# An attention and MLP kernel without its dummy matmuls, with attention re-paced and the users of v casts held back

## The chip, the cores and the metric

The kernel runs on one core of a Trainium2 chip. The metric is device time in microseconds. Every execution listed here is of state "fast", and each came with the span of the core and the mean granted TensorE clock. Before the change: 347.17 us, the median of 3 runs (346.78 to 348.75) that were known when the prediction was made.

## The reference, cut to what matters

Attention over 8 batches of 8 heads, 576 queries, head size 64, with 16 extra "beacon" keys before the 576 causal ones. Its output, as 4608 tokens of 512 numbers, goes through an MLP with a squared ReLU.

```python
# q, k, v: (8, 8, 576, 64); beacon_k, beacon_v: (8, 8, 16, 64)
scores = scale * q @ concat(beacon_k, k).T        # causal on the last 576 keys
a = softmax(scores)
x = (a @ concat(beacon_v, v)).transpose(0, 2, 1, 3).reshape(4608, 512)
h = x @ w_in                                      # 512 -> 2048
g = maximum(h, 0) ** 2
return g @ w_out                                  # 2048 -> 512
```

## The kernel before

The kernel does not write its instructions by hand in order. It lists operations with a modelled duration, dependencies and a priority. A small simulation of time (`Order.run`) then picks, for each engine, which ready operation comes next. Only the resulting order reaches the chip. A modelled number therefore never makes the chip wait; it only decides what stands before what.

Attention works on 32 pairs of heads: pair p belongs to batch p // 4. The MLP works on 9 chunks of 512 tokens. Chunk j can start once the attention of batch (512 (j+1) - 1) // 576 is normalised and transposed into `xT`: for batches 0 to 2 by TensorE, for batches 3 to 7 by a DMA transpose on the queue of SP. Other names in the traces: `stg` holds what was just loaded from memory; a cast turns it into bf16 (`vb` for v, `qk_area` for q and k); `qT` and `kT` are q and k transposed; `strip` holds scores, `pt` their exp, `xn` the normalised output before its transpose.

Dummy matmuls fill TensorE where the model has it idle before 22 us:

```python
    FILL_UNTIL = 22.0
    # ... in run(), when no operation is ready for engine e:
                    if best is None:
                        if e == "PE" and 0.3 < now < self.FILL_UNTIL and self.pools["ps"]:
                            cols = 128 if now < 4.0 else 256
                            free[e] = now + 0.107
                            issued.append((Op("fill", "PE", 0.107, ...
```

Attention is paced against the MLP. `progress` is the MLP's modelled TensorE time so far. A pair's scores may be issued only when it has reached a share of a chunk for each pair; if nothing else is ready, the gate is ignored (`fallback`):

```python
    mlp_chunk_us = 27.7
    LEAD, PACE = -0.4, 0.255
        def gate(o):
            if p < HP:
                return True
            return o.progress >= mlp_chunk_us * (LEAD + PACE * (p - HP))
```

`late` holds back TensorE's users of an operation in the model, because loads can be later on the chip than in it:

```python
        cast[b, x, c] = add(f"cast{b}{x}{c}", engs, ..., emit_cast, ...,
                            late=2.0 if x == "v" and b > 0 else 0.0)
        trans[b, x] = [add(f"tr{b}{x}", "SP", 4.1, emit, ..., dma=3.7, late=3.0)]
            o = add(f"xt{b}.{t}", "SP", 1.32, emit, ..., dma=0.64 * n / 128, late=0.5)
```

The softmax here doesn't subtract the row's maximum and nothing guards it: scores larger than these inputs give would overflow.

Of the kernel before, what the change touches and what calls it, by code (L numbers as in the profile page):

```python
# [45 lines left out]
class Order:  # L46
# [2 lines left out]

    LAT = {"PE": 0.2, "ACT": 0.2, "DVE": 0.15, "POOL": 0.25, "SP": 0.1, "-": 0.0}  # L50

    FILL_UNTIL = 22.0
    DEPTH = {"SP": 4, "ACT": 8, "POOL": 8}
    DMA_LAT = {"SP": 0.6, "ACT": 0.6, "POOL": 2.0}

# [7 lines left out]
    def add(self, *a, **kw):  # L63
        op = Op(*a, **kw)
        op.need = [d for d in op.need if d is not None]
        self.ops.append(op)
        return op

    def run(self):
        engines = ["PE", "ACT", "DVE", "POOL", "SP", "-"]  # L70
        for op in self.ops:
            op.left = len(op.need) + len(op.behind)
            for d in op.need:
                d.users.append(op)
            for d in op.behind:
                d.followers.append(op)
        avail = {e: [] for e in engines}

        def release(op):
            for e in op.engs:  # L80
                avail[e].append(op)

        for op in self.ops:
            if op.left == 0:
                release(op)
        free = {e: 2.3 if e == "DVE" else 0.0 for e in engines}
        dma_free = 0.0
        lanes = {"SP": [], "POOL": [], "ACT": []}
        events = [(0.0, 0, None, None)]
        seq = 0  # L90
        started = set()
        issued = []
        now = 0.0
        while events:
            now = events[0][0]
            while events and events[0][0] <= now + 1e-9:
                _, _, kind, op = heapq.heappop(events)
                if kind in ("done", "done_pe"):
                    for u in op.users:
                        if ("PE" in u.engs) == (kind == "done_pe"):  # L100
                            u.left -= 1
                            if u.left == 0:
                                release(u)
                elif kind == "give":
                    from_op, which = op.give if isinstance(op.give, tuple) else (op.give, 0)
                    pool, cls = from_op.take[:2]
                    self.pools[pool].append(from_op.slots[which])
                    if cls in self.inuse:
                        self.inuse[cls] -= 1
            again = True  # L110
            while again:
                again = False
                for e in engines:
                    if free[e] > now + 1e-9:
                        continue
                    best = None
                    fallback = None
                    for op in avail[e]:
                        if any(free[x] <= now + 1e-9 for x in op.engs[:op.engs.index(e)]):
                            continue  # L120
                        if op.take:
                            pool, cls, need = op.take
                            if len(self.pools[pool]) < need:
                                continue
                            if cls in self.limits and self.inuse[cls] + need > self.limits[cls]:
                                continue
                        if op.gate is not None and not op.gate(self):
                            if fallback is None or op.prio < fallback.prio:
                                fallback = op
                            continue  # L130
                        if op.dma and len(lanes[e]) >= self.DEPTH[e] and lanes[e][-self.DEPTH[e]] > now + 1e-9:
                            continue
                        if best is None or op.prio < best.prio:
                            best = op
                    if best is None:
                        best = fallback
                    if best is None:
                        if e == "PE" and 0.3 < now < self.FILL_UNTIL and self.pools["ps"]:
                            cols = 128 if now < 4.0 else 256
                            free[e] = now + 0.107  # L140
                            issued.append((Op("fill", "PE", 0.107, lambda e, cols=cols, bank=self.pools["ps"][0]: self.fill(bank, cols)), e, now))
                            seq += 1
                            heapq.heappush(events, (free[e], seq, "free", None))
                        continue
                    op = best
                    started.add(id(op))
                    for u in op.followers:
                        u.left -= 1
                        if u.left == 0:
                            release(u)  # L150
                    for ee in op.engs:
                        avail[ee].remove(op)
                    if op.take:
                        pool, cls, need = op.take
                        op.slots = [self.pools[pool].pop(0) for _ in range(need)]
                        op.held = (pool, cls, op.slots[0])
                        if cls in self.inuse:
                            self.inuse[cls] += need
                    dur = op.dur[e] if isinstance(op.dur, dict) else op.dur
                    end = now + dur  # L160
                    free[e] = end
                    self.progress += op.pe_time
                    issued.append((op, e, now))
                    seq += 1
                    heapq.heappush(events, (end, seq, "free", op))
                    if op.dma:
                        dma_free = max(dma_free, now + self.DMA_LAT[e]) + op.dma
                        seen = max(end, dma_free + 1.6)
                        lanes[e].append(seen)
                        seq += 1  # L170
                        heapq.heappush(events, (seen, seq, "free", op))
                    else:
                        seen = end + self.LAT[e]
                    seq += 1
                    heapq.heappush(events, (seen, seq, "done", op))
                    seq += 1
                    heapq.heappush(events, (seen + op.late, seq, "done_pe", op))
                    if op.give is not None:
                        seq += 1
                        heapq.heappush(events, (seen, seq, "give", op))  # L180
                    again = True
        assert len(started) == len(self.ops), [o.name for o in self.ops if id(o) not in started][:20]
        for op, e, _ in issued:
            if e != "-":
                op.insts = op.emit(e)
                for d in op.sync:
                    for x in op.insts:
                        self.wait_for(x, d.insts[-1])
        self.issued = issued
        return now  # L190
# [3 lines left out]
def kernel(  # L194
# [11 lines left out]
    nc = tc.nc  # L206
# [17 lines left out]
    def sb(name, shape, dt):  # L224
        return pool.tile(shape, dt, name=name)
# [41 lines left out]
    g = [sb(f"g{i}", [128, NFT, TCH], BF16) for i in range(2)]  # L267
# [4 lines left out]
    ps = [psum.tile([128, 512], FP32, name=f"ps{i}") for i in range(4)]  # L272

    def wait_for(later, first):
# [3 lines left out]
    order = Order(  # L278
        pools={"strip": range(2), "ps": range(4), "stg": range(NSTG), "pt": range(NPT)},
        limits={"av": 2, "tp": 2},  # L280
    )
    order.wait_for = wait_for

    def emit_fill(bank, cols):
        nc.tensor.matmul(ps[bank][:, 0:cols], g[1][:, 0, 0:128], g[1][:, 0, 0:cols], start=True, stop=True)  # L285

    order.fill = emit_fill

    add = order.add

    nc.vector.memset(g[1][:, 0, 0:256], 0.0)
    nc.vector.memset(warm, 0.0)  # L292
    for i in range(2):
        nc.vector.memset(kT[i][:, :, Nb + S:NT * 128], 0.0)
# [54 lines left out]
    def add_load(b, x, c, prio, behind=[], sync=[]):  # L349
# [34 lines left out]
        if x != "v":  # L384
            if b < NPE + 2:
                deps += [zero_ops[b]]
            else:
# [1 line left out]
        engs = ("POOL", "DVE") if b == 0 and c <= 1 else ("POOL",)  # L389
        cast[b, x, c] = add(f"cast{b}{x}{c}", engs, {"DVE": 0.6, "POOL": 0.65}, emit_cast,  # L390
                            prio=prio if b else prio - 220.0, deps=deps, give=ld,
                            late=2.0 if x == "v" and b > 0 else 0.0)

    def add_trans(b, x, prio):
        srcb, dst = (qb, qT) if x == "q" else (kb, kT)
# [57 lines left out]
    def add_strided(b, prio):  # L453
# [7 lines left out]
        for part, (t0, np_, ns, prs) in enumerate(parts_of[b]):  # L461
            n_tok = np_ * ns
            own = b == 0 and part < 2
            for pr in prs:
                groups = ["kq"] if 2 * n_tok <= 1024 else ["k", "q"]
                for n, xs in enumerate(groups):
                    box = {}

                    def emit_tp(e, xs=xs, pr=pr, box=box, part=part, np_=np_, ns=ns, n_tok=n_tok, own=own, prs=prs):
                        pp = ps[box["t"].held[2]].bitcast(BF16)  # L470
                        for i, x in enumerate(xs):
                            for u in range(ns):
# [6 lines left out]
                                                        strided_buf(b, x, part)[:, 2 * (pr - prs[0]) + hj, u, :],  # L479
                                                        ident[0:np_, 0:np_])  # L480

                    tp = add(f"tp{b}.{part}.{pr}{xs}", "PE", 0.1 + (0.055 if b == 0 else 0.075) * ns * len(xs), emit_tp,
                             prio=100.0 * (HP * b + pr) - (190 if b else 1190 if part == 0 else 1090) + 0.1 * n,
                             deps=[strided[b, part, pr, x] for x in xs] + [ident_op], take=("ps", "tp"))
                    box["t"] = tp
# [95 lines left out]
        return SPLIT if p < NSPLIT else WHOLE  # L581

    mlp_chunk_us = 27.7
    LEAD, PACE = -0.4, 0.255
    norm_ops = {}

    def add_pair(b, pr):
# [291 lines left out]
    late = []  # L879
    for b in range(B):  # L880
# [3 lines left out]
        if b < NPE:  # L884
            add_strided(b, lp - 200.0 if b == 0 else lp)
# [31 lines left out]
        if b >= 1:  # L917
            for j in late:
                add_chunk(j)
            late = []  # L920
# [48 lines left out]
```

## Time and profile before

| what | before | where it is read |
|---|---|---|
| median of the runs | 347.17 us | the runs |
| span of the profiled execution | 347.5 us | the page |
| TensorE busy | 334.9 us, 96% | the page, part 1 |
| waits for xT | 0.57 and 1.92 us | waits, timeline |
| half clock in the middle | 3.41 us | clock records, windows |
| dummy matmuls | 71, 10.6 us busy | the page, part 5 |

The page of the kernel before: TensorE in 40 slices (tenths busy), its granted clock in tenths, and the chain of work that ended last by engine and by line.

```profile
PE   8899999999999999999999998999999999999995
...
PEclk9999999999999999999999999899999999999999
...
PE 83%; DMA 6%; DVE 3%; POOL 3%; SPq 2%; issue 1%; ACT 1%; ACTq 0%; POOLq 0%; DVEq 0%
PE ps L805 34%; PE ps L840 33%; PE ps L674 8%; PE strip L622 7%; DMA stg<-in_v_dram 4%; DMA xT<-xn 2%; POOL qk_area L443 1%; PE ps L742 1%; SPq L365 1%; DVE pt L648 1%; DVE pt L651 1%; SPq L725 1%; PE ps L478 1%; POOL vb L320 0%; DVE xn L694 0%
```

Two thirds of the chain are the two MLP matmul lines, L805 (x times w_in) and L840 (g times w_out). TensorE is what the kernel is made of, so a gain can only come from its holes. One slice of the clock row shows an 8.

The waits of TensorE before (who waited for what: us in total, times, longest):

```profile
PE ps L805 <- DMA xT<-xn: 2.5, 2, 1.9
...
PE ps L674 <- POOL vb L320: 0.8, 3, 0.4
```

The timeline of TensorE before, around the longest of them (start, busy time, engine, line, shapes and count; in brackets the idle time before it and what ended that):

```profile
213.53 0.63 PE L674 MATMUL ps<-vb,pt 128*128 128x65 bf16 x15
214.09 0.58 PE L622 MATMUL strip<-qT,kT 64*128 64x496 bf16 x4
214.60 1.04 PE L840 MATMUL ps<-w_out,g 128*128 128x512 bf16 x4
217.55 3.55 PE L805 MATMUL ps<-xT,w_in 128*128 128x512 bf16 x8 [1.92 <-DMA xT<-xn]
221.03 0.48 PE L622 MATMUL strip<-qT,kT 64*128 64x336 bf16 x8
```

TensorE sits idle for 1.92 us until xT of batch 5 lands. Then eight matmuls take 3.55 us. The windows view before shows why. Its columns are the stretch, its length, the busy time of PE, PEld, DVE, ACT and POOL with their counts, the granted clock (PEclk), the DMA share and GB/s.

```profile
214.12:217.54 3.42, 1.52 (x10) 0.41 (x9) 1.38 (x3) 2.07 (x3) 0.99 (x2) 1.00 1.39 97
217.54:220.95 3.41, 3.40 (x8) 1.00 (x8) 0.69 (x1) 0.00 (x0) 0.00 (x0) 0.50 0.68 190
220.95:224.36 3.41, 3.36 (x22) 1.63 (x23) 2.48 (x5) 2.61 (x5) 0.00 (x0) 1.00 1.10 228
```

A stretch of 3.42 us with TensorE busy for 1.52 us is followed by 3.41 us at half clock, and that by full clock again.

The start before, in TensorE's timeline: one group of 24 attention-times-v matmuls, and the first MLP matmuls.

```profile
19.75 0.91 PE L674 MATMUL ps<-vb,pt 128*128 128x65 bf16 x24
...
24.19 0.57 PE L805 MATMUL ps<-xT,w_in 128*128 128x240 bf16 x4
```

### The profile page before, as it was taken

Reading aid. Unit: us, or ns where it says so; the run is one execution under the profiler, and the core shown is the slowest. Engines: PE = TensorE matmul, PEld = TensorE weight load, DVE = VectorE, ACT = ScalarE, POOL = GpSimd, SP = SyncE. Lnnn points to the kernel's source line nnn. Section 1 sums busy time; section 2 is a strip of 40 time slices with the busy share of each in tenths; the row PEclk is TensorE's granted clock in tenths of the full one; section 3 lists DMA queues with packets and bytes.
Section 4 is the critical chain, followed back from the end, with each engine's and each line's share of the span. In section 5 each row is a group of like instructions: output and inputs, shape, how many; then the busy total and the mean of one; then the engine's idle time right before and its main releaser. Section 6 shows DMA issues by size and latency. Waiting matters only on the chain.

```text
span 347.5 us, 7286 instructions
## 1 busy us (share of the span) xinstructions
PE 334.9 (96%) x2916; PEld 179.9 (52%) x2957; DVE 169.0 (49%) x366; ACT 193.9 (56%) x293; POOL 92.2 (27%) x144
## 2 busy tenths in 40 slices
PE   8899999999999999999999998999999999999995
PEld 7578765444554544444458743444444454444442
DVE  6696974258436862467246733473256412301300
ACT  3787764377656744576437644475467616615611
POOL 9674803316315515210423054021000000000000
PEclk9999999999999999999999999899999999999999
DMA  8999979999999999698989999990520032011002
GB/s 143 207 206 211 205 122 203 235 213 214 200 229 217 220 196 210 144 208 134 206 137 238 223 210 154 225 210 2 106 85 2 0 104 87 2 60 61 2 24 97
DMA packets 143664, 51.70 MB, mean 149 GB/s; under 512 B 130670, under 2 KB 138382, under 8 KB 143630
## 3 DMA queue, kind: packets, MB, share of 16 engines
q1 hardware_dynamic: 135231, 42.25, 61.7%
q0 software_dynamic: 7904, 8.69, 14.8%
q8 instruction: 23, 0.38, 0.5%
q10 hardware_dynamic: 495, 0.30, 0.3%
q14 instruction: 11, 0.09, 0.1%
HBM read 37.22 MB, written 9.44 MB: 134 GB/s over the span
## 4 chain that ended last, share of the span: by engine, by line
PE 83%; DMA 6%; DVE 3%; POOL 3%; SPq 2%; issue 1%; ACT 1%; ACTq 0%; POOLq 0%; DVEq 0%
PE ps L805 34%; PE ps L840 33%; PE ps L674 8%; PE strip L622 7%; DMA stg<-in_v_dram 4%; DMA xT<-xn 2%; POOL qk_area L443 1%; PE ps L742 1%; SPq L365 1%; DVE pt L648 1%; DVE pt L651 1%; SPq L725 1%; PE ps L478 1%; POOL vb L320 0%; DVE xn L694 0%
## 5 line engine op out<-in xcount | busy, mean ns | idle before, releaser
L805 PE MATMUL ps<-xT,w_in 128*128 128x512 bf16 (+3 forms) x689 | 134.6, 343 | 3.3 <-DMA xT<-xn 2.5
L840 PE MATMUL ps<-w_out,g 128*128 128x512 bf16 x550 | 130.5, 379 | 1.8 <-issue 0.8
L637 ACT ACTIVATE pt<-strip 128x832 bf16<-128x832 f32 (+4 forms) x128 | 103.9, 863 | 28.9 <-PE strip L622 28.4
L805 PEld LDWEIGHTS <-w_in 128*128 128x128 bf16 x704 | 65.3, 98 | 59.2 <-issue 9.4
L821 ACT ACTIVATE g<-ps 128x512 bf16<-128x512 f32 (+2 forms) x123 | 68.4, 556 | 45.9 <-PE ps L805 45.0
L840 PEld LDWEIGHTS <-g 128*128 128x128 bf16 x576 | 52.5, 98 | 61.8 <-issue 4.4
L830 DVE TENSOR_TENSOR g<-g 128x1024 bf16<-128x1024 bf16 (+2 forms) x80 | 51.0, 642 | 58.6 <-ACT g L821 57.2
L318 ACT COPY osb<-ps 128x512 f32<-128x512 f32 x32 | 18.8, 586 | 66.5 <-PE ps L840 45.6
L320 POOL CAST qk_area<-stg 128x512 bf16<-128x512 f32 (+2 forms) x60 | 39.5, 665 | 59.0 <-DMA stg<-in_k_dram 39.1
L320 POOL CAST vb<-stg 128x512 bf16<-128x512 f32 (+1 forms) x39 | 26.6, 693 | 78.0 <-DMA stg<-in_v_dram 57.1
L674 PEld LDWEIGHTS <-pt 128*128 128x128 bf16 (+1 forms) x960 | 37.1, 97 | 15.6 <-issue 3.9
L674 PE MATMUL ps<-vb,pt 128*128 128x65 bf16 (+1 forms) x960 | 40.5, 194 | 2.0 <-POOL vb L320 0.8
L648 DVE TENSOR_TENSOR pt<-pt,tri 128x1024 bf16<-128x1024 bf16 (+1 forms) x36 | 24.6, 686 | 29.9 <-ACT pt L637 29.9
L622 PE MATMUL strip<-qT,kT 64*128 64x80 bf16 (+6 forms) x400 | 35.0, 277 | 0.2 <-DMA kT<-qk_area 0.2
L692 DVE RECIPROCAL rcp<-ps 128x5 f32<-128x5 f32 (+2 forms) x64 | 12.3, 193 | 41.8 <-PE ps L674 41.5
L694 DVE TENSOR_TENSOR xn<-ps,rcp 128x320 bf16<-128x320 f32 (+2 forms) x64 | 31.5, 492 | 2.3
L823 DVE TENSOR_SCALAR g<-ps 128x512 bf16<-128x512 f32 (+2 forms) x37 | 23.4, 632 | 16.1 <-PE ps L805 14.7
L622 PEld LDWEIGHTS <-kT 64*128 64x128 bf16 x400 | 11.9, 94 | 18.0 <-issue 13.9
L651 DVE TENSOR_TENSOR pt<-pt,tri 80x160 bf16<-80x160 bf16 x32 | 12.2, 383 | 0.0
L285 PE MATMUL ps<-g 128*128 128x256 bf16 (+1 forms) x71 | 10.6, 298 | 1.1 <-DVE warm L292 1.1
L365 POOL DMA_DIRECT2D stg<-in_v_dram x10 | 8.5, 852 | 4.9 <-DMA w_in<-in_moe_w_in_dram 3.4
L285 PEld LDWEIGHTS <-g 128*128 128x128 bf16 x71 | 6.7, 121 | 2.7 <-DVE warm L292 1.1
(41 smaller groups left out, 70.4 us busy)
## 6 DMA issues: line engine op xcount, KB each, us to landing
out_dram<-osb SPq DMA_DIRECT2D x17, 512.0 KB, 3.3
stg<-in_q_dram SPq DMA_DIRECT2D x24, 256.0 KB, 4.9
stg<-in_k_dram SPq DMA_DIRECT2D x18, 256.0 KB, 5.2
stg<-in_v_dram SPq DMA_DIRECT2D x18, 256.0 KB, 5.3
w_in<-in_moe_w_in_dram POOLq DMA_DIRECT2D x4, 512.0 KB, 9.2
w_out<-in_moe_w_out_dram POOLq DMA_DIRECT2D x4, 512.0 KB, 10.8
stg<-in_v_dram POOLq DMA_DIRECT2D x6, 256.0 KB, 8.8
stg<-in_k_dram SPq DMA_DIRECT2D x6, 224.0 KB, 3.9
```

Of the source, the lines that this page charges most:

```text
L318: nc.scalar.copy(dst, src)
L320: eng[e].tensor_copy(dst, src)
L622: nc.tensor.matmul(st[:, hj, at:at + t1 - t0], kT[b % 2][hp, pr, 128 * c:128 * c + 128], qT[b % 2][hp, pr, t0:t1], start=True, stop=True,)
L637: nc.scalar.activation(pt[take_pt.held[2]][:, :, off:off + width], st[:, :, 0:width], AF.Exp, bias=0.0, scale=scale)
L648: nc.vector.tensor_tensor(out=d, in0=d, in1=tri[:, m0:m0 + m, :][:, None].to_broadcast([128, 2, m, 128]), op=ALU.min)
L674: nc.tensor.matmul(a[:, at + (t - tl[0]) * (D + 1):at + (t - tl[0] + 1) * (D + 1)], P[0:rr, hj, o:o + 128], vb[b % 2][0:rr, c, 2 * pr + hj ...
L694: nc.vector.tensor_tensor(out=xn[b % 2].rearrange("p t (h d) -> p h t d", d=D)[:, h0:h0 + nh, tl[0]:tl[0] + nt], in0=a[:, :, :, 0:D], in1= ...
L805: nc.tensor.matmul(h[:, lo - spans[0][0]:hi - spans[0][0]], w_in_sb[:, mc, ft * 128:(ft + 1) * 128], xT[:, mc, lo % RING:lo % RING + hi - lo],
L821: nc.scalar.activation(dst, h, AF.Relu, bias=0.0, scale=1.0)
L823: nc.vector.tensor_scalar(out=dst, in0=h, scalar1=0.0, scalar2=None, op0=ALU.max)
L830: nc.vector.tensor_tensor(out=d, in0=d, in1=d, op=ALU.mult)
L840: nc.tensor.matmul(o, G[:, fc, ts * 128:(ts + 1) * 128], w_out_sb[:, fc, :], start=(fc == 0), stop=(fc == NFT - 1))
```

## The change

The intent: take out the dummies; let attention run a little ahead of where it did, by a smaller step of MLP progress per pair; and place TensorE's users of v casts later in the order. The modelled cost of the transposes of batch 0 also goes up, because they no longer run on a clock that dummies have raised.

```diff
-    FILL_UNTIL = 22.0
... (run) ...
-                        if e == "PE" and 0.3 < now < self.FILL_UNTIL and self.pools["ps"]:
-                            ... a dummy matmul of 128 or 256 columns, 0.107 us ...
... (casts) ...
-                            late=2.0 if x == "v" and b > 0 else 0.0)
+                            late=5.0 if x == "v" and b > 0 else 0.0)
... (transposes on TensorE) ...
-                    tp = add(..., "PE", 0.1 + (0.055 if b == 0 else 0.075) * ns * len(xs), emit_tp,
+                    tp = add(..., "PE", 0.1 + (0.1 if b == 0 else 0.075) * ns * len(xs), emit_tp,
... (pace) ...
-    LEAD, PACE = -0.4, 0.255
+    LEAD, PACE = -0.4, 0.245
```

The emitter of the dummies and the memset of their operand go too.

## The prediction

> **What bounds the kernel now.** TensorE. The page has PE busy 334.9 of 347.5 us (96%), and the chain that ended last lies 83% on PE, 67% on the two MLP lines (L805, L840). By the timeline, PE is nearly gap-free from 24.2 us (first MLP matmul) on. Three kinds of loss are left:
>
> 1. Start, 0 to 24 us. PE does not bind: exp on ACT runs back to back from 9.4 to 16.3 us; the first attention-times-v matmuls wait for v casts until 16.57, those for loads. 71 dummy matmuls (10.6 us busy) fill PE's holes. The clock records show full clock from 5.91 us.
> 2. Two waits for the transposed attention output (DMA xT<-xn): 0.57 us at 142.75 and 1.92 us at 217.55. After the second the clock records show 0.5 for 3.41 us (217.54 to 220.95): eight L805 matmuls start 427 ns apart instead of 216, another 1.7 us. The 3.4 us before held about 1.5 us of matmuls. The Trainium skill (TensorE: Matmul & The Clock Gate, The HAM clock gate) describes this: a free-running window of 3413 ns, half clock after an idle one. The trace agrees on the 3.413 us, but here a window about half idle was enough.
> 3. Waits for v casts or masks at 41.5 and 107 us: 0.38 + 0.35 + 0.24 us.
>
> **What the change moves.** I compared the two orders of PE's instructions, summing matmul columns at full clock. PACE moves attention forward, by 2 us near pair 13, 5 us near pair 22, 7 us near pair 28. The PE work between a batch's last v product and the first MLP matmul that reads it grows: chunk 3 from 10.9 to 13.3 us, chunk 4 from 11.8 to 15.0, chunk 5 (the 1.92 us wait) from 10.9 to 18.4, chunk 6 from 10.1 to 18.5. So both xT waits should go, and the half clock with them: 1.92 + 1.70 + 0.57 = 4.2 us. The larger hold-back moves the first v products of batches 1, 2 and 3 later by 2.4, 1.5 and 0.9 us of PE work: up to 0.9 us more. Batches 4 to 7 run earlier, against v casts that ended 5.1, 4.1, 7.8 and 15.8 us before use; I keep 0.5 us for new waits.
>
> **What the removal costs.** From 4.2 to 24.2 us there are about 13 us of real PE work at full clock. Without fill, the first transposes and scores run at half clock, and the stretch 12.7 to 16.2 us, which holds about 1.3 us of real matmuls, should drop the clock again just as PE catches up (6.3 us of work from 16.6 to 24.2). A half-clock window with 3.4 us of demanded work costs at most 1.7 us. I estimate the first MLP matmul 1.5 to 3 us later (2.3 in the sum), at worst 5.
>
> **Sum.** -4.2 -0.9 +0.5 +2.3 = -2.3 us: 344.9 us, range 341.5 to 349. Chances: faster by over 2% 0.04, within 0.93, slower 0.03.
>
> **What would show it.** Right: no half clock near 217 us, no wait for xT<-xn over 0.5 us; clock records with half clock inside 4 to 24 us; first L805 at 25 to 26.5 us. Wrong: first L805 before 24.5 or after 28 us; new PE waits for kT, vb or xT over 1 us in all; another half-clock stretch after 30 us.
>
> **What would make it wrong.** The loads may not follow the earlier attention (DMA is 90% busy until about 235 us), or a new half-empty stretch of 3.4 us costs its own 1.7 us.

## More of the kernel before

Why xT was late stands in two places. The last normalised output of batch 5 (timeline of VectorE before, one line):

```profile
205.47 0.49 DVE L694 TENSOR_TENSOR xn<-ps,rcp 128x320 bf16<-128x320 f32 x1
```

and the queue of SP, which issued these DMAs one after another (timeline of SP before):

```profile
206.38 1.03 SPq L365 DMA_DIRECT2D stg<-in_q_dram  x1
207.50 3.14 SPq L365 DMA_DIRECT2D stg<-in_k_dram  x3
210.73 7.30 SPq L725 DMA_TRANSPOSE xT<-xn  x5
```

The output is ready at 205.96 us; its transposes are issued from 210.73 us on, 4.8 us later, behind a row of loads. The second of the five, the last that chunk 5 needs, lands at 217.42 us.

## The result and the profile after

343.46 us, median of 5 runs (342.63 to 343.79), against 347.17 us (346.78 to 348.75, 5 runs). The ratio is 0.9878, with a 95% interval of 0.9849 to 0.9907. (A ratio here is the mean time of one kernel's fast runs over that of the other's of the same rounds, so not quite the ratio of the medians quoted.) A second job, below, gave 0.9899. The change is a gain of about 1.1%, which is inside the 2% band.

Line numbers after are 13 lower: L792 is L805 of before, L827 is L840, L661 is L674, L712 is L725. The page after, same rows:

```profile
PE   4999999999999999999999999999999999999995
...
PEclk9999999999999999999999999999999999999999
...
PE 85%; DMA 8%; POOL 3%; DVE 2%; ACT 0%; issue 0%; SPq 0%; POOLq 0%; ACTq 0%
```

TensorE's waits after, all that the view lists:

```profile
PE ps L462 <- DVE qk_area L307: 4.9, 2, 4.3
PE strip L609 <- DMA kT<-qk_area: 0.4, 1, 0.4
PE ps L661 <- DVE vb L307: 0.3, 1, 0.3
PE ps L792 <- DVE qT L307: 0.2, 1, 0.2
```

The waits for xT are gone. The same place in TensorE's timeline after:

```profile
214.71 0.62 PE L661 MATMUL ps<-vb,pt 128*128 128x65 bf16 x15
215.26 0.58 PE L609 MATMUL strip<-qT,kT 64*128 64x496 bf16 x4
215.78 2.76 PE L792 MATMUL ps<-xT,w_in 128*128 128x512 bf16 x12
```

and SP's timeline after:

```profile
206.54 7.06 SPq L712 DMA_TRANSPOSE xT<-xn  x5
```

and the last normalised output of batch 5 after, in VectorE's timeline:

```profile
198.61 0.49 DVE L681 TENSOR_TENSOR xn<-ps,rcp 128x320 bf16<-128x320 f32 x1
```

TensorE was ready for the MLP chunk at 215.64 us before and starts it at 215.78 us after. The consumer has not moved. Attention of batch 5 is done 6.9 us earlier (199.10 us against 205.96), but the transposes are issued only 4.2 us earlier (206.54 against 210.73): they now stand 7.4 us behind loads in SP's queue, not 4.8. The second of them lands at 211.03 us, 4.8 us before it is needed. Whether issuing the transposes ahead of those loads would have done the same was not tested.

The start after, TensorE's timeline:

```profile
4.31 0.83 PE L462 MATMUL ps<-ident,qk_area 120*128 120x120 bf16 x4 [4.31 <-DVE qk_area L307]
...
18.44 1.50 PE L661 MATMUL ps<-vb,pt 128*128 128x65 bf16 x24
...
23.99 0.57 PE L792 MATMUL ps<-xT,w_in 128*128 128x240 bf16 x4
```

The group of 24 that took 0.91 us before takes 1.50 us. The clock records after begin only at 22.47 us, with full clock; the page counts a stretch without a record as full clock, so the row of nines does not show what the durations show. By these durations TensorE ran at half clock from its first matmul until 22.47 us, and yet the first MLP matmul comes at 23.99 us, 0.2 us earlier than in the profile before.

### The profile page after: what moved, and what is told of

It is laid out like the page before. It is cut to its first block, busy times and chain, and to the rows that moved or that the text cites. A ratio compares the mean times of both kernels' runs of the same rounds, so it can differ in the third digit from the quotient of the medians.

```text
span 342.1 us, 7180 instructions
## 1 busy us (share of the span) xinstructions
PE 332.1 (97%) x2886; PEld 176.4 (52%) x2886; DVE 169.4 (50%) x371; ACT 191.9 (56%) x287; POOL 92.5 (27%) x144
## 4 chain that ended last, share of the span: by engine, by line
PE 85%; DMA 8%; POOL 3%; DVE 2%; ACT 0%; issue 0%; SPq 0%; POOLq 0%; ACTq 0%
PE ps L792 34%; PE ps L827 34%; PE ps L661 8%; PE strip L609 7%; DMA stg<-in_v_dram 3%; DMA kT<-qk_area 2%; DMA stg<-in_q_dram 2%; DMA stg<-in_k_dram 1%; POOL qk_area L430 1%; PE ps L729 1%; POOL qk_area L307 1%; DVE qT L307 1%; DVE g L817 0%; PE ps L465 0%; POOL tri L291 0%
## 5 line engine op out<-in xcount | busy, mean ns | idle before, releaser
L827 PE MATMUL ps<-w_out,g 128*128 128x512 bf16 x576 | 133.8, 379 | 0.0
L792 PE MATMUL ps<-xT,w_in 128*128 128x512 bf16 (+3 forms) x704 | 133.4, 341 | 0.2 <-DVE qT L307 0.2
L792 PEld LDWEIGHTS <-w_in 128*128 128x128 bf16 x704 | 65.7, 98 | 56.4 <-issue 4.3
L808 ACT ACTIVATE g<-ps 128x512 bf16<-128x512 f32 (+2 forms) x119 | 67.0, 563 | 41.6 <-PE ps L792 40.9
L827 PEld LDWEIGHTS <-g 128*128 128x128 bf16 x576 | 52.7, 98 | 60.9 <-issue 3.2
L817 DVE TENSOR_TENSOR g<-g 128x1024 bf16<-128x1024 bf16 (+2 forms) x80 | 52.5, 659 | 61.8 <-ACT g L808 59.5
L305 ACT COPY osb<-ps 128x512 f32<-128x512 f32 x28 | 16.4, 585 | 57.4 <-PE ps L827 51.3
L661 PEld LDWEIGHTS <-pt 128*128 128x128 bf16 (+1 forms) x960 | 37.8, 100 | 14.8 <-issue 3.5
L661 PE MATMUL ps<-vb,pt 128*128 128x65 bf16 (+1 forms) x960 | 41.5, 197 | 0.3 <-DVE vb L307 0.3
L609 PE MATMUL strip<-qT,kT 64*128 64x80 bf16 (+6 forms) x400 | 37.3, 292 | 0.4 <-DMA kT<-qk_area 0.4
L307 DVE COPY osb<-ps 128x512 f32<-128x512 f32 x8 | 5.5, 692 | 19.1 <-PE ps L827 19.0
L638 DVE TENSOR_TENSOR pt<-pt,tri 80x160 bf16<-80x160 bf16 x32 | 10.3, 320 | 0.0
L307 DVE COPY kT<-ps 128x576 bf16<-128x576 bf16 (+3 forms) x11 | 6.5, 594 | 1.9 <-PE ps L465 1.0
```

The lines of the kernel that those rows point to most:

```text
L305: nc.scalar.copy(dst, src)
L307: eng[e].tensor_copy(dst, src)
L609: nc.tensor.matmul(st[:, hj, at:at + t1 - t0], kT[b % 2][hp, pr, 128 * c:128 * c + 128], qT[b % 2][hp, pr, t0:t1], start=True, stop=True,)
L661: nc.tensor.matmul(a[:, at + (t - tl[0]) * (D + 1):at + (t - tl[0] + 1) * (D + 1)], P[0:rr, hj, o:o + 128], vb[b % 2][0:rr, c, 2 * pr + hj ...
L792: nc.tensor.matmul(h[:, lo - spans[0][0]:hi - spans[0][0]], w_in_sb[:, mc, ft * 128:(ft + 1) * 128], xT[:, mc, lo % RING:lo % RING + hi - lo],
L808: nc.scalar.activation(dst, h, AF.Relu, bias=0.0, scale=1.0)
```

## The experiments

Twelve runs were made, two of them repeats (a1_after, b1_before); all gave correct results. Each was timed beside the kernel before. The four of a job share one chip and the same 11 runs of before, so times are compared inside a job first.

The theory at the outset: the gain comes from the pace alone, by more TensorE work between a batch's last attention-times-v matmul and the first MLP matmul that reads its xT ("the distance", counted in the order of the instructions, with each matmul's columns at full clock); the half clock at the start costs little because the start is bound elsewhere. The rivals: the dummies themselves held the kernel back; or v casts were what stalled TensorE.

### One part of the change at a time

**k1_nofill**: the dummies go, nothing else is edited. (The order of the real instructions in the first 35 us shifts with it, since the model no longer has TensorE busy with dummies.)

```diff
 (the changed kernel, with the other parts undone)
-    LEAD, PACE = -0.4, 0.245
+    LEAD, PACE = -0.4, 0.255
-                            late=5.0 if x == "v" and b > 0 else 0.0)
+                            late=2.0 if x == "v" and b > 0 else 0.0)
-                    tp = add(..., 0.1 + (0.1 if b == 0 else 0.075) * ns * len(xs), ...
+                    tp = add(..., 0.1 + (0.055 if b == 0 else 0.075) * ns * len(xs), ...
```

> Only the dummy matmuls go; pace 0.255, hold-back 2.0 and the modelled transpose cost stay as before. Theory (the start is bound by loads and exp, so a half-clock start costs little, and the gain of the change comes from the pace): half clock until about 22 us, first MLP matmul within 1 us of 24.2, the xT wait near 217 us and its half-clock stretch still there; 346.5 to 348.5 us, ratio 0.998 to 1.004. Rival (the dummies themselves held the kernel back, and their removal is the gain): 343 to 344.5 us, ratio below 0.993.

**k2_pace**: the pace alone.

```diff
 (the kernel before)
-    LEAD, PACE = -0.4, 0.255
+    LEAD, PACE = -0.4, 0.245
```

> Only the pace, 0.255 to 0.245; dummies and hold-back stay. Theory: both waits for xT and the half-clock stretch near 217 us vanish; gain 3.3 to 4.2 us, so 343.0 to 344.0 us, ratio 0.988 to 0.991. Rival (gain from the removed dummies or from the hold-back): ratio above 0.995.

**k3_late**: the hold-back of v users alone.

```diff
 (the kernel before)
-                            late=2.0 if x == "v" and b > 0 else 0.0)
+                            late=5.0 if x == "v" and b > 0 else 0.0)
```

> Only the hold-back of the users of v casts, 2.0 to 5.0. Theory: removes the 0.35 + 0.24 us waits near 107 us and part of the 0.38 us near 41.5, nothing else: gain 0.3 to 1 us, ratio 0.997 to 0.999, the 217 us wait stays. Rival (v casts are what stalls TensorE): gain over 2 us.

**k5_fillback**: all of the change except that the dummies stay.

```diff
 (the kernel before)
-                            late=2.0 ...          +  late=5.0 ...
-    ... (0.055 if b == 0 else 0.075) ...          +  ... (0.1 if b == 0 else 0.075) ...
-    LEAD, PACE = -0.4, 0.255                      +  LEAD, PACE = -0.4, 0.245
```

> All of the change but the dummies kept (61 of them are placed). Theory (half-clock start costs nothing): 342.5 to 344.5 us, within 1 us of the changed kernel. Rival (the changed kernel's start is bound by TensorE at half clock from 16 to 22.5 us): first MLP matmul 1 to 2 us earlier than 24.0, 341.5 to 342.5 us.

| kernel | median us (6 runs) | range | ratio to before | 95% interval |
|---|---|---|---|---|
| before, same job | 346.23 (11 runs) | 343.27 to 348.37 | | |
| k1_nofill | 345.57 | 344.81 to 346.56 | 0.9992 | 0.9946 to 1.0038 |
| k2_pace | 343.63 | 343.10 to 344.46 | 0.9937 | 0.9891 to 0.9982 |
| k3_late | 347.27 | 346.45 to 348.28 | 1.0041 | 0.9990 to 1.0092 |
| k5_fillback | 343.95 | 343.55 to 345.07 | 0.9950 | 0.9904 to 0.9996 |

The pace alone reaches 343.63 us, close to the whole change in its own jobs (343.46 and 343.72). That is a comparison across jobs. By the ratios the pace alone has 0.9937 and the whole change 0.9878 and 0.9899; the intervals overlap, so it is not shown that the pace is all of the gain, only that it gains; what the rest adds cannot be told from these runs. Taking the dummies out is worth nothing that can be told from zero. In the profile of k1_nofill the first MLP matmul is at 24.22 us, the clock records begin at 21.29 us, and the wait for xT is still there. It is 0.5 us long in this execution and has no half clock after it. From TensorE's waits of k1_nofill, that line alone:

```profile
PE ps L792 <- DMA xT<-xn: 0.5, 1, 0.5
```

TensorE's waits of k2_pace, all but the one for the first instruction:

```profile
PE ps L674 <- POOL vb L320: 1.0, 3, 0.6
```

With the pace alone there is no wait for xT. The waits for v casts stay, as they should: the hold-back is at its old value. In size the theory asked for more than came: it expected a ratio of 0.988 to 0.991, and the interval of 0.9891 to 0.9982 only just reaches it, though the time itself lies inside the expected 343.0 to 344.0. A likely reason is the yardstick: before ran from 343.27 to 348.37 us, and the theory had been sized on one slow execution of it (below).

The hold-back alone did not gain the expected 0.3 to 1 us. It was 0.4% slower, with an interval that includes zero. In its profile the v casts are no longer waited for at 107 us, but chunk 3 now waits for xT, and half clock follows. TensorE's timeline of k3_late:

```profile
140.00 1.04 PE L840 MATMUL ps<-w_out,g 128*128 128x512 bf16 x4
143.00 1.35 PE L805 MATMUL ps<-xT,w_in 128*128 128x512 bf16 x4 [1.97 <-DMA xT<-xn]
144.15 1.91 PE L840 MATMUL ps<-w_out,g 128*128 128x512 bf16 x4
```

Four L840 matmuls took 1.04 us before the wait and 1.91 us after it. The windows of k3_late there, columns as before:

```profile
140.15:143.56 3.41, 1.44 (x7) 0.52 (x6) 0.16 (x1) 1.65 (x2) 1.06 (x2) 1.00 0.63 122
143.56:146.97 3.41, 3.41 (x16) 1.09 (x14) 0.69 (x1) 0.87 (x2) 0.00 (x0) 0.50 0.28 59
```

All six runs of k3_late have a mean clock of 0.993 to 0.995, which fits one such stretch each. A later attention is not the reason: the output of batch 3 is normalised at 131.35 us here, in before at 132.72 and 132.06 (second profile). But the transposes, behind SP's loads, are issued at 137.25 us, against 137.53 and 136.75. TensorE was ready for chunk 3 at 141.03 us, against 142.18 and 141.52: it came earlier and the transposes did not, so the distance for chunk 3, unchanged at 10.9 us, was no longer enough. That is read from three profiles, not tested on its own.

k5_fillback, at 343.95 us, has the time of the changed kernel in its jobs (343.46 and 343.72) within what the runs can tell, although its dummies did not even keep the clock up: the records show half clock from 11.14 to 17.96 us, after a stretch with TensorE waiting 0.19, 0.94 and 0.11 us for loads of q and k. Its first MLP matmul is the latest of all profiles, 25.45 us. The rival of that run, an earlier start, did not appear.

### The distance, from the other side

**a1_after**: the changed kernel again, as the yardstick of this job.

> The changed kernel again, beside the next three on the same chip. Ratio to before 0.988 to 0.995: before varied from 343.3 to 348.4 us in the runs so far, so the ratio depends on how often before meets its long waits for xT.

**m1_xtlate**: the kernel before, with the MLP held back instead of attention brought forward.

```diff
 (the kernel before)
-            o = add(f"xt{b}.{t}", "SP", 1.32, ..., dma=0.64 * n / 128, late=0.5)
+            o = add(f"xt{b}.{t}", "SP", 1.32, ..., dma=0.64 * n / 128, late=14.0)
```

> Before with one number changed: TensorE's users of the DMA-transposed xT are held back 14 us instead of 0.5 in the model of time. The attention's order, the pace, the dummies and the v hold-back stay. PE work between a batch's last v product and the first MLP matmul on it: chunks 3 to 6 from 10.9, 11.8, 10.9, 10.1 us to 16.0, 16.7, 14.7, 15.0. Theory (the pace gains only through that distance): no wait for xT over 0.5 us, no half clock after 30 us, 343 to 344.5 us, as with the pace alone (343.6). Rival (an earlier attention is what gains, by less contention late): ratio above 0.996.

**m3_pace26**: the changed kernel with the pace moved the other way.

```diff
 (the changed kernel)
-    LEAD, PACE = -0.4, 0.245
+    LEAD, PACE = -0.4, 0.26
```

> The changed kernel with the pace 0.26 instead of 0.245: attention later. Distance for chunks 3 to 7: 10.9, 9.2, 7.9, 5.7, 3.5 us of PE work. Theory: about 13 us are needed, so waits for xT of about 1 to 2 us at chunk 3 growing to 4 to 6 us at chunk 6, with a half-clock stretch (1.7 us) after most of them: 352 to 365 us. Rival (distance does not matter): within 2 us of before.

| kernel | median us (6 runs) | range | ratio to before | 95% interval |
|---|---|---|---|---|
| before, same job | 347.66 (11 runs) | 345.07 to 349.21 | | |
| a1_after | 343.72 | 343.43 to 343.96 | 0.9899 | 0.9864 to 0.9934 |
| m1_xtlate | 356.00 | 355.89 to 358.77 | 1.0272 | 1.0229 to 1.0314 |
| m3_pace26 | 350.37 | 348.31 to 352.57 | 1.0098 | 1.0049 to 1.0148 |

m3_pace26 goes the way of the theory, with three waits for xT (1.68 us at 145.06, 1.06 at 182.55 and 1.29 at 219.10), and 4 of its 6 runs have a mean clock of 0.994 or 0.995. From TensorE's waits of m3_pace26:

```profile
PE ps L792 <- DMA xT<-xn: 4.0, 3, 1.7
```

The size was wrong: 352 to 365 us was expected. The expectation took one needed distance, 13 us, for all chunks. But chunk 6, with a distance of 5.7 us, did not wait at all. The chunks do not need the same amount. In this profile it takes 11.9, 10.2, 8.6 and 4.6 us from the end of the batch's last v product to the landing of the last transpose that chunk 3, 4, 5 and 6 needs; their distances are 10.9, 9.2, 7.9 and 5.7 us, so the first three wait and the fourth does not. What differs most is SP's queue: the transposes are issued 6.6, 4.6, 3.0 and 0.8 us after that v product. For chunk 6, loads no longer stand in front of them. The number of transposes is the lesser part: chunks 3 and 4 need three of five, chunks 5 and 6 two.

m1_xtlate is the miss. Its distances for chunks 3 to 6 are 3.8 to 5.1 us longer than before, and the waits for xT are gone, as the theory said. But it is 2.7% slower. From TensorE's waits of m1_xtlate:

```profile
PE strip L622 <- ACT pt L637: 7.4, 16, 1.0
PE ps L674 <- DVE pt L648: 1.6, 5, 0.4
```

When the MLP is held back, the model finds nothing but attention for TensorE, and its gate lets attention through when nothing else is ready. So score matmuls stand back to back without MLP work between them, and each waits until exp on ScalarE frees a buffer. One wait of 1 or 2 us was traded for 16 of up to 1 us. Half clock came too, against the expectation: 3.41 us of it from 260.90 us on, after a stretch of 3.42 us (257.48 to 260.90) in which TensorE was busy for 1.38 us and no single gap was over 0.95 us. All six runs have a mean clock of 0.984 to 0.995. So a longer distance only gains when something useful fills it: the producer must come earlier, the consumer must not just go later. This also means that m1_xtlate did not test what it was made for, since the attention's order did not stay as it was.

### The start

**m2_warm**: the changed kernel with its order of real instructions kept on each engine, plus dummies where its model has TensorE idle.

```diff
 (the changed kernel)
-        for op, e, _ in issued:
+        pe_end = 1.2
+        for op, e, at in issued:
+            if e == "PE":
+                if op.take and op.take[0] == "ps" and at < 22.0:
+                    for _ in range(max(0, int((at - pe_end) / 0.107))):
+                        self.fill(op.slots[0], 128 if at < 4.3 else 256)
+                pe_end = at + 0.6 * op.dur
 (and the dummies' emitter and memset, as before)
```

> The changed kernel, its instruction order kept on every engine, with 58 dummy matmuls put only where its model has TensorE idle before 22 us. Theory (half clock at the start costs about 0.5 to 1 us of the final time): 0.3 to 1.0 us below the changed kernel in this batch, first MLP matmul near 23.1 us, full clock from about 6 us. Rival (the start is bound elsewhere, the clock costs nothing): within 0.2 us of it.

Measured in the same job as a1_after: 343.56 us (342.50 to 344.66), ratio 0.9895 (interval 0.9858 to 0.9933). Against 343.72 us that is no difference. Yet the start was quicker: the first MLP matmul at 23.03 us against 23.73. Adding up matmul columns at full clock, m2_warm is 1.4 us ahead by the point that a1_after reaches at 69.2 us. It then loses that again. TensorE's timeline of m2_warm:

```profile
68.64 2.32 PE L803 MATMUL ps<-xT,w_in 128*128 128x512 bf16 x10
72.64 0.58 PE L620 MATMUL strip<-qT,kT 64*128 64x496 bf16 x4 [1.68 <-DMA kT<-qk_area]
```

The first scores of batch 2 wait 1.68 us for kT. This is the point at which the start's gain is given back. kT of batch 2 comes out of a chain of loads, casts and a DMA transpose. From SP's timeline of m2_warm:

```profile
49.18 0.31 SPq L362 DMA_DIRECT2D stg<-in_beacon_k_dram  x1
...
61.13 3.17 SPq L396 DMA_TRANSPOSE qT<-qk_area  x1
...
65.01 3.90 SPq L396 DMA_TRANSPOSE kT<-qk_area  x1
```

The kernel makes the loads of batch 2 wait for the last w_out load. In all 14 profiles (before, after and the twelve runs) the first load of batch 2 was issued 0.07 or 0.08 us after w_out had landed, which was between 48.7 and 50.5 us. kT landed between 69.3 and 74.5 us, and the first scores of batch 2 started between 71.0 and 74.5 us. The five profiles with a cold start lie inside that range (72.2 to 73.9 us).

But the loads alone do not explain the wait of m2_warm. Its kT transpose was issued at 65.01 us, 0.55 us before that of a1_after (65.56), and landed 1.2 us after it (72.60 against 71.41): 7.59 us from issue to landing instead of 5.85. In the five cold profiles it took 5.85 to 6.00 us, in seven of the nine with dummies 7.04 to 7.70, in the other two 5.95 (t3_warm_tr5_p24) and 4.92 (k5_fillback). Why is open.

The last job tried to close the argument by giving TensorE more to do before those scores.

**t1_cold_tr5** and **t2_warm_tr5**: users of the kT and qT transposes held back 5.0 us, without and with the dummies of m2_warm. **t3_warm_tr5_p24**: the latter with the pace 0.24. **b1_before**: the kernel before, for a second profile.

```diff
 (t1: the changed kernel; t2, t3: m2_warm)
-        trans[b, x] = [add(f"tr{b}{x}", "SP", 4.1, emit, ..., dma=3.7, late=3.0)]
+        trans[b, x] = [add(f"tr{b}{x}", "SP", 4.1, emit, ..., dma=3.7, late=5.0)]
 (t3 also)
-    LEAD, PACE = -0.4, 0.245
+    LEAD, PACE = -0.4, 0.24
```

> The kernel before, unchanged, for a second profile. The half-clock stretch after 30 us stood in the first profile of before, but the clock column shows 0.993 to 0.995 in only 7 of the 22 runs of before so far. Expected: 345 to 349 us; a wait for xT between 0.3 and 2 us at chunk 3 or chunk 5; the half-clock stretch there only if the wait is near 2 us.

> The changed kernel with users of the kT and qT transposes held back 5.0 us instead of 3.0: TensorE has 1.8 us more work before its first scores of batch 2. Theory (kT of batch 2, landing near 71.5 us by its loads, decides the time there in the warm variant; the changed kernel with its half-clock start just arrives with it): 0 to 0.4 us below the changed kernel (343.6), so 343.2 to 343.7. Rival (the half-clock start is simply free): same, so this run is the control for the next.

> The same hold-back of 5.0 us with the 58 dummies in the order of the changed kernel. Theory (what the full clock gains at the start, 1.4 us by 60 us, is lost again in the 1.68 us wait for kT at 72.6 us): that wait is under 0.4 us, and the kernel is 0.8 to 1.5 us below the cold variant: 342.0 to 342.8 us. Rival (the start's gain is lost anyhow): within 0.3 us of the cold variant.

> The previous one with the pace 0.24. Distances for chunks 3 to 6 grow beyond what chunk 5 needed, so no gain is expected from them: within 0.4 us of the previous one, or slower by up to 1 us if attention comes too early for its loads.

| kernel | median us | range | ratio to before | 95% interval |
|---|---|---|---|---|
| before, same job | 346.70 (11 runs) | 344.15 to 348.39 | | |
| b1_before | 345.93 (4 runs) | 344.65 to 347.74 | 0.9997 | 0.9941 to 1.0053 |
| t1_cold_tr5 | 344.27 (6 runs) | 342.85 to 344.79 | 0.9940 | 0.9897 to 0.9983 |
| t2_warm_tr5 | 344.18 (6 runs) | 343.29 to 345.56 | 0.9943 | 0.9895 to 0.9991 |
| t3_warm_tr5_p24 | 343.66 (6 runs) | 342.87 to 344.17 | 0.9926 | 0.9884 to 0.9968 |

The expected gain of t2_warm_tr5 over t1_cold_tr5, 0.8 to 1.5 us, did not come. In its profile there was no lead to keep: the first MLP matmul is at 23.73 us, in t1_cold_tr5 at 23.38. It also still shows TensorE waiting for kT, 0.85 us of it for batch 2, since in that execution w_out landed at 50.49 us and kT at 74.47, 3.1 us later than in a1_after (71.41). It waits 0.8 us for xT as well, in two waits. From TensorE's waits of t2_warm_tr5:

```profile
PE strip L620 <- DMA kT<-qk_area: 1.2, 2, 0.8
```

So it is shown that the warm start's lead was lost in a wait for kT in one profile of m2_warm, and that no warm variant was clearly faster in its runs. That the lead could be kept by moving those scores later is not shown; t2_warm_tr5, with 1.8 us of extra work, was no test of it. None of the runs is clearly faster than the changed kernel, which was not itself in this job.

b1_before gives the second look at before. The two largest of its TensorE waits:

```profile
PE ps L674 <- POOL vb L320: 1.5, 2, 0.9
PE ps L805 <- DMA xT<-xn: 1.4, 2, 0.9
```

The same two waits for xT, shorter (0.47 us at 141.99 and 0.93 us at 215.77), and no half clock after them. Its span is 344.1 us where that of the first profile is 347.5. In the 37 runs of before that have a clock in these three jobs, a mean clock of 0.993 to 0.995, which is what one 3.41 us stretch at half speed makes of 345 us (0.5 x 3.41 / 345 = 0.005), stands in 9. Their mean time is 348.3 us, and that of the other 28 is 345.9 us. None of the 11 runs of the changed kernel has it (0.997 to 1.0), nor any of k2_pace.

## Why the prediction was right, and where it was not

The time was predicted at 344.9 us (341.5 to 349), within 2%; it came out at 343.46. The range was wide: the unchanged kernel, at 347.17 us, lies in it too. Step by step:

1. **TensorE bounds the kernel and only its holes can be won: right.** Nothing but holes changed; the chain stays 83 to 85% on TensorE.
2. **Both waits for xT go, through the pace: right.** The profile of k2_pace, without the rest of the change, shows it, and m3_pace26 shows the waits growing when attention is moved the other way. After the change the transposes of batch 5 are issued 4.2 us earlier for a consumer that starts at the same time. What the prediction left out is that they first stand behind loads in SP's queue, which took 2.7 us of the 6.9 that attention gained.
3. **"1.92 + 1.70 + 0.57 = 4.2 us": right in kind, mis-sized.** The terms were read from one execution of before, which turned out to be a slow one (span 347.5 us; the second profile has 344.1). The half-clock stretch, 1.70 us of the sum, was in 9 of 37 runs, so on average it is worth 0.24 x 1.70 = 0.4 us. The waits were 1.4 us in the second profile instead of 2.5. The pace alone measured 346.23 - 343.63 = 2.6 us in medians, in its job.
4. **The hold-back gives up to 0.9 us: not confirmed.** Alone it measured 1.0041, with a wait for xT in place of those for v. Within the full change its share cannot be told from zero: the pace alone has 343.63 us, the full change 343.46 and 343.72 in other jobs. It was not taken out of the full change by itself.
5. **The missing dummies cost 2.3 us: wrong, and this is the step that failed.** Both halves of it failed. The clock was expected to rise early, fall again near 16 us and recover; it stayed at half until 20.5 to 22.5 us in each of the five cold profiles. And that much longer half clock cost less: in the five cold profiles the first MLP matmul is at 23.4 to 24.2 us, in the eight whose dummies had raised the clock by 10.5 us it is at 23.0 to 24.2. The difference of the means is 23.85 - 23.43 = 0.4 us, with ranges that overlap, instead of 1.5 to 3. The one pair with the same order of instructions, a1_after and m2_warm, has 23.73 and 23.03: 0.7 us. (k5_fillback, which had dummies and yet fell to half clock, is left out: 25.45 us, after waits for loads.) The 24.19 us from which the prediction counted is itself the latest of the eight; in that execution the second tile of v landed at 16.03 us, the latest of all 14 (13.35 to 16.03). On the final time, k1_nofill shows nothing (0.9992, and its interval, up to 1.0038, leaves no room for 1.5 us). The prediction's own test, a first MLP matmul before 24.5 us, called this wrong, and so it was.

The sum was near by luck, because two errors had opposite signs: too much gain from one slow sample of before (4.2 + 0.9 - 0.5 = 4.6 us forecast, 2.6 measured for the pace alone), too much cost for the cold start (2.3 us forecast, 0.4 at the first MLP matmul and none that shows in the time).

What the step overlooked was stated in the prediction itself: that TensorE does not bind before 24 us. At half clock TensorE fills its holes with the same work, more slowly. What is then left of the delay can vanish where kT of batch 2 is waited for. One profile, that of m2_warm, shows such a wait take back the lead of a warm start. That it does so in every execution is not shown: the profiles of k2_pace and t3_warm_tr5_p24, warm too, have no wait for kT. Known is only that the times of the runs do not differ.

## What to carry to other kernels

A wait is removed by bringing its producer forward far enough, and only if other work fills the time in between; holding the consumer back without such work makes new waits. To know how far, follow the producer's whole way: here the transposes of batch 5 stood 4.8 us behind loads in a DMA queue before the change, and 7.4 us after it. Dummy work that kept the clock up in a start with many waits gained nothing here that the times could show. And when a kernel's runs differ by 1% among themselves, size a gain on several profiles or on the runs' own clocks, not on the one profile at hand.

## What the Trainium skill lacked or had wrong

- "TensorE: Matmul & The Clock Gate" (The HAM clock gate) says that the clock halves after at least one idle window of about 3.4 us, and its table of rules (Why this matters for your kernels) asks for no idle gaps over about 3 us. The window's length agrees (3.413 us in the records), but here gaps of 1.92 and 1.97 us were enough, when they fell into one window that left TensorE busy for 1.52 and 1.44 us of 3.4. In m1_xtlate no gap was over 0.95 us, and a window with TensorE busy for 1.38 us of 3.42 did it. A gap of 1.68 us in m2_warm, in a window with TensorE busy for 2.00 us of 3.42, did not do it; but in k5_fillback a window busy for 2.17 us of 3.41 (7.73 to 11.14), mostly transposes and scores, did. So the busy time of a window does not settle it alone. The page tells of clocks that fall with frequent short idles, but gives no limit for a partly busy window.
- The same page says that full clock comes after about 3.4 us of sustained work. In the profile after, TensorE's busy time is 7.58 us of the 8 from 12 to 20 us, and full clock came at 22.47 us, 18 us after the first matmul. The work in between is transposes, scores on 64 rows and short matmuls of 65 columns. Its section "PE-mode transpose" says that transposes do not count as busy in the same way; the runs here do not contradict that, but no run tells which part of the work did not count.
- In these profiles the clock records begin with the first change of the clock, and a stretch before it is shown as full clock; after the change this hides 18 us at half clock, which only the durations show (1.50 us for 24 matmuls that take 0.91). The same page warns not to trust single clock events fully; it does not name this.
- "TensorE: Matmul & The Clock Gate" (Why this matters for your kernels) advises keeping TensorE busy to get past the half clock. It does not say when that does not pay: in this start, with waits for loads and casts in it, dummy work for it gained nothing that shows (ratio 0.9992 without the dummies, interval 0.9946 to 1.0038).
